# Second product of the experts as seven products of halves in the second and third group, with split weights kept in device memory by the first group

## The chip, the core and the metric

The kernel runs on one core of one Trainium2 chip. The metric is device time in microseconds (us) of one execution. The engines of a core work side by side, each through its own list of instructions in order: TensorE (PE in the profile, with its weight loads shown apart as PEld), VectorE (DVE), ScalarE (ACT), GpSimd (POOL) and SyncE (SP), which here does little more than issue transfers (DMAs). They wait for each other through semaphores.

## The reference, cut to what matters

An attention-like stage without softmax and a three-matrix bilinear stage make `x` (2304 tokens of 512). The last stage, four experts, is what the change is about:

```python
p = domain_probs / (domain_probs.sum(-1, keepdims=True) + 1e-09)
out = np.zeros((N, D), dtype=np.float32)            # N = 2304, D = 512
for e in range(E):                                   # E = 4 experts
    h = np.maximum(x @ w1[e], 0.0)                   # w1[e]: 512 x 1024
    out += p[:, e:e + 1] * (h @ w2[e])               # w2[e]: 1024 x 512
```

All of it is float32. The kernel gets there with three matmuls for each product of two tiles: every operand is split into a high part, rounded to the format that TensorE takes, and a low part, the rest; high x high, high x low and low x high are summed.

## The kernel before

**Tiles.** Everything is cut into tiles of 128 partitions and up to 512 float32 columns (256 KB). 99 such buffers (pool `h`) stay in the core's memory, 5 larger ones (pool `r`, 4 KB a partition) take loads, and 8 banks of 128x512 (pool `b`) take what PE sums.

**The expert stage.** The tokens form three groups `g` = 0, 1, 2 (the first, second and third) of 768 each, as two halves of `W` = 384 tokens or `TILES3` = 3 tiles. For each group, each expert `e` and each `i` = 0..3 there is one step:

- `expert_weights(e, i)` loads 512 KB of each weight matrix (tiles `e1raw`, `e2raw`) and splits them. For `w1` it first makes four sums and differences of quarter blocks (`winograd_weights`, `combined`, line 949; tiles `s12`, `s34`), so that the first product can be done with seven products of halves instead of eight. High parts are casts (line 332, mostly ACT), low parts subtractions (line 337, DVE or POOL).
- `up(g, e, i)` does the first product: seven products of 6 matmuls 128x384, 42 in all. Their results are added up by DVE (tiles `u`, line 1065); `relu` then writes the high part of relu(u) (line 1074) and its low part (line 1086): tiles `ht`.
- `down(g, e, f)` for f = i and f = i + 4 does the second product: for each of 2 x 3 tiles of tokens three matmuls 128x512 (lines 284 to 286), summed over the eight f in six banks. An expert has 8 x 6 x 3 = 144 of these in each group.
- `collect` (line 1145) adds each bank, times the share of the expert, to one of six tiles `acc`; after the last expert `store` writes them out.

All weights are loaded, combined and split anew in each of the three groups.

**The order.** The kernel lists all operations with the engines that could do them and a guessed duration for each. `Plan.order` then walks through a simulated time: each free engine takes, of the operations whose inputs are ready and whose buffers can be had, the one with the lowest stage number, up to `WINDOW` = 14 stages ahead. A stage is one entry of `items`: one `up` or one `down` here, and `mixed(b, f)`, one step of the product ahead of the experts. `down` of a step stands behind `up` of the next. The result fixes the order on each engine; on the chip each engine runs its list in that order.

**Places ahead of the experts.** `mixed` (matmuls `abh,w3oh`) ends in the tiles `xf`; `group_operands(g)` makes from these the 14 split operands `x11`, `x21`, `x22`, `t1` to `t4` of a group (28 tiles).

Of the kernel before, what the change touches and what calls it, by code (L numbers as in the profile page):

```python
# [22 lines left out]
RINGS = {"attention": 9, "decoded": 6}  # L23
WINDOW = 14
WARM = 10
START = 0.7
# [18 lines left out]
class Pair:  # L45
# [7 lines left out]
    def __getitem__(self, at):  # L53
        return self.high[at], self.low[at]


# [164 lines left out]
def attention_moe_kernel(  # L221
# [23 lines left out]


    nc = tc.nc
    B, H, S, D = q.shape
# [51 lines left out]
    def t_pe(n, passes=3):  # L300
        return passes * (0.0137 + n / 2400)

    def load(buf, *parts, key=None, queue="sp", cost=None):
# [11 lines left out]
    def spilled(name, buf):  # L315

        d = Buf("d", name, [P, 512], F32, tag=name)
        add(
            {"sp": 0.73}, lambda _: nc.sync.dma_start(out=d[:, :], in_=buf.tile),
            reads=[buf], writes=[d], latency=2.4,  # L320
        )
        return d

    def whole(t):
        return t

    def split(dst, src, n, to=whole, value=whole, psum=False, key=None):
# [8 lines left out]
        def low(e):  # L336
# [9 lines left out]
            {"dve": t_dve(n)} if psum else {"dve": t_dve(n), "pool": t_pool(n)}, low,  # L346
            reads=[src, (dst.high, key)], writes=[(dst.low, key)], free=psum,
        )

# [640 lines left out]
    def winograd_weights(raw1, full=False):  # L990
# [15 lines left out]
        combined("s4", 256, a12, own(s12, 256), ALU.subtract, [raw1, (s12, 256)], s34, hi)  # L1006
        wa, wb, wc, wd = (Pair("we") for _ in range(4))
        split(wa, raw1, 512, whole, lambda t: t[:, 0])
        if full:
            split(wb, raw1, 512, whole, lambda t: t[:, 1])  # L1010
        else:
            split(wb, raw1, 256, lambda t: t[:, 0:256], lambda t: t[:, 1, 256:512])
        split(wc, s12, 512)
# [5 lines left out]
    def expert_weights(e, i):  # L1019
# [13 lines left out]
        return w, dict(zip(fs, downs))  # L1033

    operands = {}
# [5 lines left out]
    def up(g, e, i):  # L1041
        if g not in operands:
            operands[g] = group_operands(g)
        x = operands[g]
        w, downs = expert_weights(e, i)
        for f, d in downs.items():
            we2[g, e, f] = d

# [19 lines left out]

        def relu(f, part, src):
            s = hts[g, e, f, part] = Pair("ht")  # L1070

# [49 lines left out]
    def down(g, e, f, first, last):  # L1121
# [3 lines left out]
        for i in range(2):  # L1125
            s = hts[g, e, f, i]
            for t in range(TILES3):
# [6 lines left out]
                if last:  # L1134
                    collect(e, *token_tile(g, i, t), ps)

    def collect(e, b, t, ps):
        if e == 0:
# [17 lines left out]
        )  # L1156
        if e < NE - 1:
            return

        def store(_):  # L1160
            if b < B:
# [49 lines left out]
    for b in range(1, NB):  # L1211
        for f in range(KF):
            item(mixed, b, f)
    steps = [(g, e, i) for g in range(len(GROUPS)) for e in range(NE) for i in range(KF // 2)]
    for n, (g, e, i) in enumerate(steps + [(None,) * 3]):
        if g is not None:
            item(up, g, e, i)
        if n:
            g, e, i = steps[n - 1]
            item(down, g, e, i, i == 0, False)  # L1220
            item(down, g, e, i + KF // 2, False, i == KF // 2 - 1)

# [42 lines left out]
```

## Time and profile before

| | |
|---|---|
| time, median of 3 runs | 1158.21 us (1155.22 to 1158.61) |
| the profiled execution: its own time | 1157.3 us |
| its span from the first to the last instruction | 1155.5 us |
| PE busy | 1142.5 us, 99% of the span |
| DVE, ACT, POOL busy | 808.1, 501.8 and 280.7 us |
| moved by DMA | 108.06 MB, mean 94 GB/s |
| PE among the chain of work that ended last | 95% |

The three lines of the second product (284 to 286, 128x512) are the costliest groups on PE. A PE row gives the duration of one matmul from its start to its modelled end; consecutive matmuls overlap, so the pace has to be read from the distance between starts. A row of idle time names what ended it.

### The profile page before, as it was taken

What the parts mean: (1) busy time and instruction counts of PE and PEld (TensorE: products, weight loads), DVE (VectorE), ACT (ScalarE), POOL (GpSimd) and SP (SyncE); (2) the same over time, 40 slices, a digit from 0 to 9 for tenths busy, and PEclk for the clock granted to TensorE, in tenths of its full rate; (3) what the DMA queues carried; (4) which work ended last, traced back from release to release, by engine and by line L of the source; (5) the groups of instructions that cost most, each with busy time, mean ns of one, the idle gap of its engine ahead of it and who ended that gap; (6) DMA issues with size and microseconds to landing.
All of it is one profiled execution on the core that took longest, in us unless ns stands there. A gap on an engine that the chain in (4) does not pass through costs nothing.

```text
span 1155.5 us, 16373 instructions
## 1 busy us (share of the span) xinstructions
PE 1142.5 (99%) x6036; PEld 1011.6 (88%) x6036; DVE 808.1 (70%) x1434; ACT 501.8 (43%) x996; POOL 280.7 (24%) x250
## 2 busy tenths in 40 slices
PE   7999999999999999999999999999999999999998
PEld 6888888888888999989999988999998999998887
DVE  4887787788622676678677886668678987576833
ACT  5776763354434533433335444333333444333210
POOL 3435671033300600001012640001015831010200
PEclk8999999999999999999999999999999999999999
DMA  9996513235200222221121442122120532121001
GB/s 272 330 320 191 172 34 106 75 118 198 85 1 1 82 65 74 73 74 60 55 69 37 128 128 73 41 70 73 55 73 18 166 106 77 55 73 55 1 1 55
DMA packets 108784, 108.06 MB, mean 94 GB/s; under 512 B 13216, under 2 KB 82848, under 8 KB 108704
## 3 DMA queue, kind: packets, MB, share of 16 engines
q1 hardware_dynamic: 107488, 106.75, 29.7%
q8 instruction: 47, 0.77, 0.3%
q10 hardware_dynamic: 1216, 0.26, 0.1%
q14 instruction: 33, 0.27, 0.1%
HBM read 93.88 MB, written 13.11 MB: 93 GB/s over the span
## 4 chain that ended last, share of the span: by engine, by line
PE 95%; DMA 2%; DVE 1%; SPq 0%; ACT 0%; issue 0%; DVEq 0%
PE b L286 31%; PE b L285 30%; PE b L284 30%; PE b L621 2%; PE b L677 1%; PE b L649 1%; DMA kvr<-in_v_dram 1%; DMA kvr<-in_k_dram 1%; DMA w1raw<-in_moe_w_dram 0%; DMA q<-in_q_dram 0%; DVE acc L1145 0%; PE b L714 0%; SPq L306 0%; DVE tl L337 0%; DVE wel L337 0%
## 5 line engine op out<-in xcount | busy, mean ns | idle before, releaser
L1065 DVE TENSOR_TENSOR u<-u,b 128x384 f32<-128x384 f32 x336 | 180.8, 552 | 189.9 <-PE b L286 170.4
L286 PE MATMUL b<-wdh,htl 128*128 128x512 f32 x576 | 225.6, 392 | 0.0
L285 PE MATMUL b<-wdl,hth 128*128 128x512 f32 x576 | 225.4, 391 | 0.0
L284 PE MATMUL b<-wdh,hth 128*128 128x512 f32 x576 | 224.1, 389 | 0.0
L1074 ACT ACTIVATE hth<-u 128x384 fp32r<-128x384 f32 x192 | 100.7, 526 | 221.1 <-DVE u L1065 220.9
L1086 DVE SCALAR_TENSOR_TENSOR htl<-u,hth 128x384 fp32r<-128x384 f32 x192 | 122.2, 640 | 9.9 <-ACT hth L1074 5.0
L609 ACT COPY u<-b 128x384 f32<-128x384 f32 (+1 forms) x76 | 39.6, 521 | 204.1 <-PE b L286 199.5
L286 PEld LDWEIGHTS b<-wdh,htl 128*128 128x128 f32 x576 | 108.0, 188 | 22.7
L285 PEld LDWEIGHTS b<-wdl,hth 128*128 128x128 f32 x576 | 108.1, 188 | 19.1
L284 PEld LDWEIGHTS b<-wdh,hth 128*128 128x128 f32 x576 | 108.2, 188 | 18.9
L332 ACT CAST weh<-s 128x512 fp32r<-128x512 f32 x112 | 68.7, 617 | 43.7 <-DVE s L949 41.1
L337 DVE TENSOR_TENSOR wel<-s,weh 128x512 fp32r<-128x512 f32 x92 | 70.3, 791 | 8.0 <-ACT weh L332 7.0
L337 POOL TENSOR_TENSOR wel<-e1raw,weh 128x256 fp32r<-128x256 f32 (+1 forms) x22 | 37.0, 1681 | 134.8 <-PE b L285 53.5
L337 POOL TENSOR_TENSOR wdl<-e2raw,wdh 128x512 fp32r<-128x512 f32 x17 | 25.3, 1491 | 178.4 <-PE b L286 118.9
L332 ACT CAST wdh<-e2raw 128x512 fp32r<-128x512 f32 x96 | 57.8, 616 | 8.8 <-DMA e2raw<-in_moe_w_dram 6.4
L284 PE MATMUL b<-abh,w3oh 128*128 128x512 f32 (+1 forms) x160 | 59.4, 371 | 0.0
L286 PE MATMUL b<-abh,w3ol 128*128 128x512 f32 (+1 forms) x160 | 58.9, 368 | 0.0
L285 PE MATMUL b<-abl,w3oh 128*128 128x512 f32 (+1 forms) x160 | 58.9, 368 | 0.0
L337 DVE TENSOR_TENSOR wdl<-e2raw,wdh 128x512 fp32r<-128x512 f32 x79 | 55.7, 733 | 0.0
L949 POOL TENSOR_TENSOR s<-e1raw 128x256 f32<-128x256 f32 x29 | 26.0, 906 | 90.6 <-PE b L285 89.2
L337 DVE TENSOR_TENSOR wel<-e1raw,weh 128x256 fp32r<-128x256 f32 (+1 forms) x74 | 47.7, 662 | 0.0
L332 ACT CAST weh<-e1raw 128x512 fp32r<-128x512 f32 x96 | 45.7, 509 | 4.1 <-DMA e1raw<-in_moe_w_dram 2.6
(227 smaller groups left out, 2720.8 us busy)
## 6 DMA issues: line engine op xcount, KB each, us to landing
e1raw<-in_moe_w_dram SPq DMA_DIRECT2D x96, 256.0 KB, 3.2
e2raw<-in_moe_w_dram SPq DMA_DIRECT2D x96, 256.0 KB, 2.9
w3raw<-in_moe_w_dram SPq DMA_DIRECT2D x16, 512.0 KB, 3.8
q<-in_q_dram SPq DMA_DIRECT2D x16, 256.0 KB, 5.8
kv<-in_k_dram SPq DMA_DIRECT2D x16, 256.0 KB, 5.6
kv<-in_v_dram SPq DMA_DIRECT2D x16, 256.0 KB, 5.5
w1raw<-in_moe_w_dram SPq DMA_DIRECT2D x8, 512.0 KB, 6.5
w2raw<-in_moe_w_dram SPq DMA_DIRECT2D x8, 512.0 KB, 6.8
```

What stands on the lines that cost most here:

```text
L284: nc.tensor.matmul(ps, w[0], x[0], start=first, stop=False, skip_group_check=more)
L285: nc.tensor.matmul(ps, w[0], x[1], start=False, stop=False, skip_group_check=more)
L286: nc.tensor.matmul(ps, w[1], x[0], start=False, stop=last, skip_group_check=more)
L332: nc.scalar.copy(to(dst.high.tile), value(src.tile))
L337: (nc.vector if e == "dve" else nc.gpsimd).tensor_tensor(out=to(dst.low.tile), in0=value(src.tile), in1=to(dst.high.tile), op=ALU.subtract)
L609: lambda e: nc.scalar.copy(to(dst.tile), value(src.tile)) if e == "act"
L621: nc.tensor.transpose(ps[:, c], raw[:, c], ident)
L649: nc.tensor.matmul(ps[c, c], a, b_, start=r == 0, stop=r == R)
L949: eng.tensor_tensor(out=t[:, c], in0=x, in1=y, op=op)
L1065: lambda _: nc.vector.tensor_tensor(out=t[:, :W], in0=base[:, :W], in1=ps[:, :W], op=op),
L1074: nc.scalar.activation(out=s.high[:, :W], in_=src[:, :W], func=ACTF.Relu)
L1086: lambda _: nc.vector.scalar_tensor_tensor(out=s.low[:, :W], in0=src[:, :W], scalar=0.0, in1=s.high[:, :W], op0=ALU.max, op1=ALU.subtract,),
```

## The change

In the second and third group (`g` = 1, 2) the second product is done like the first, with seven products of halves instead of eight, and the weights are no longer split there but read back.

- The first group works as before, and also writes its split `w1` tiles to device memory (`spilled`, 7 tiles of 256 KB a step; the two quarter-width parts of one pair now share a tile, `Packed`), and the split parts of `w2` that the seven products need (`keep_w2`, 768 KB a step).
- `w2_sums`, 16 entries set between those of `mixed`, loads `w2` once more, makes its four sums and differences (tiles `t12`, `t34`), splits them and writes them out: 512 KB read and 1 MB written each.
- In the second and third group `kept_weights` reads the 7 tiles `we` of a step back. `relu` works in place on `u` and splits nothing.
- `down_product(g, e, n)`, n = 0..6: reads two buffers `w2` of 512 KB (pool `r`), makes the left operand for the four `i` (`tokens_operand`: up to four sums of `u` tiles a step, and a split of each operand), and runs 3 tiles x 4 i x 3 = 36 matmuls 128x256. Seven of them replace the 144 matmuls 128x512: 252 matmuls of half the width. The four banks stay open over the seven products, and after each product `collect_half` adds three half tiles, 128x256, to `acc`: 21 in place of 6.
- The seven products of an expert are spread over the four `up` steps of the next expert; at the change from the second to the third group three stand ahead of the first `up` (`AHEAD` = 3), and the last seven stand alone at the end.

```diff
+class Packed:
+        self.tile_ = Buf("h", name, [P, 512], F32R)
+    def __getitem__(self, at):
+        _, c = at
+        return self.tile_[:, c], self.tile_[:, c.start + 256:c.stop + 256]
...
@@ def expert_weights(e, i):
         w, _ = winograd_weights(raw1)
+        tiles = [t for pair in dict.fromkeys(pair for pair, _ in w.values()) for t in pair.parts]
+        w1_kept[e, i] = [spilled(f"we{e}_{i}_{n}", t, lambda t: t.bitcast(F32)) for n, t in enumerate(tiles)]
         downs = []
         for n in range(2):
             downs.append(Pair("wd"))
             split(downs[n], raw2, 512, whole, lambda t, n=n: t[:, n])
+            for part, t in enumerate(downs[n].parts):
+                keep_w2(e, i, ((0, 1), (1, 3))[n], part, t)
...
+    W2_OPERANDS = ("b11", "b21", "b22", "t1", "t2", "t3", "-t4")
...
+    def w2_sums(e, i):
+        raw = Buf("r", "e2raw", [P, 2, 512], F32)
+        load(raw, *(
+            (lambda t, n=n: t[:, n], e_w2[e][f * P:(f + 1) * P, :]) for n, f in enumerate((i, i + KF // 2))
+        ))
...
+        combined("t1", 256, part(0, 1), part(0, 0), ALU.subtract, [raw], t12, lo)
+        combined("t2", 256, part(1, 1), own(t12, 0), ALU.subtract, [raw, (t12, 0)], t12, hi)
+        combined("t3", 256, part(1, 1), part(0, 1), ALU.subtract, [raw], t34, lo)
+        combined("-t4", 256, part(1, 0), own(t12, 1), ALU.subtract, [raw, (t12, 256)], t34, hi)
+        for t, which in ((t12, (3, 5)), (t34, (5, 7))):
+            s = Pair("wt")
+            split(s, t, 512)
+            for n, p in enumerate(s.parts):
+                keep_w2(e, i, which, n, p)
+    def kept_weights(e, i):
+        for d in w1_kept[e, i]:
+            t = Buf("h", "we", [P, 512], F32R)
+            load(t, (lambda t: t.bitcast(F32), d))
...
@@ def up(g, e, i):
-        w, downs = expert_weights(e, i)
+        if g:
+            w = kept_weights(e, i)
+        else:
+            w, downs = expert_weights(e, i)
...
         def relu(f, part, src):
+            if g:
+                h32[g, e, f, part] = src
+                add(
+                    {"act": t_act(W), "dve": t_fast(W)},
+                    lambda eng: nc.scalar.activation(out=src[:, :W], in_=src[:, :W], func=ACTF.Relu)
...
+                return
...
+    PRODUCTS = [
+        ("a11", "b11", 0, True, [(0, 0)]),
+        ("a12", "b21", 1, True, [(0, 0)]),
+        ("s2", "t2", 0, False, [(0, 1)]),
+        ("s1", "t1", 1, True, [(1, 1)]),
+        ("s3", "t3", 0, False, [(1, 1)]),
+        ("s4", "b22", 1, False, [(0, 1)]),
+        ("a22", "-t4", 0, False, [(1, 0)]),
+    ]
...
+    def down_product(g, e, n):
+        left, right, at, start, targets = PRODUCTS[n]
+        if n == 0:
+            yacc[g, e] = [[bank(), bank()] for _ in range(2)]
+        banks = yacc[g, e][at]
...
+        for i0 in range(0, KF // 2, 2):
+            raw = Buf("r", "w2", [P, 2, 2, 256], F32R)
+            add(
+                {"sp": 1.46},
+                lambda _, raw=raw, i0=i0: nc.sync.dma_start(out=raw.tile.bitcast(F32), in_=kept.tile[:, k, i0:i0 + 2]),
+                reads=[kept], writes=[raw], latency=2.4,
+            )
...
+            def mms(_, t=t, ps=ps, c=c):
+                for i, (h, (raw, r)) in enumerate(zip(lefts, rights)):
+                    mm3(
+                        ps[:, c], h[:, t * P:(t + 1) * P], (raw[:, r, 0], raw[:, r, 1]),
+                        start and i == 0 and t % 2 == 0, i == KF // 2 - 1, True,
+                    )
...
+    for g in range(1, len(GROUPS)):
+        for e in range(NE):
+            if e == 0 and g > 1:
+                for late in waiting[:AHEAD]:
+                    item(*late)
+                waiting = waiting[AHEAD:]
+            for i in range(KF // 2):
+                item(up, g, e, i)
+                n = -(-len(waiting) // (KF // 2 - i))
+                for late in waiting[:n]:
+                    item(*late)
+                waiting = waiting[n:]
+            waiting = [(down_product, g, e, n) for n in range(len(PRODUCTS))]
+    for late in waiting:
+        item(*late)
```

**On PE, second group, behind an `up` step** (names: `x22`, an operand of the group; `wd`, split `w2`; `ht`, split tokens; `b`, a bank). Before:

```order
L286 MATMUL b_8835<-x22h_6511,wel_8577 128x384
L284 MATMUL b_8847<-wdh_8122,hth_8656 128x512
L285 MATMUL b_8847<-wdl_8425,hth_8656 128x512
L286 MATMUL b_8847<-wdh_8122,htl_8667 128x512
L284 MATMUL b_8854<-wdh_8122,hth_8656 128x512
```

After:

```order
L300 MATMUL b_9317<-x22h_7141,we_9119 128x384
L298 MATMUL b_9328<-w2_9123,hth_8883 128x256
L299 MATMUL b_9328<-w2_9123,hth_8883 128x256
L300 MATMUL b_9328<-w2_9123,htl_9063 128x256
L298 MATMUL b_9328<-w2_9123,hth_8890 128x256
L299 MATMUL b_9328<-w2_9123,hth_8890 128x256
L300 MATMUL b_9328<-w2_9123,htl_9067 128x256
L298 MATMUL b_9328<-w2_9145,hth_8997 128x256
```

The matmuls are half as wide, and a bank's tile is now finished over the four `i` at once before the next tile begins.

**On SP, where the third group begins** (`we`, a kept `w1` tile read back; `w2`, a kept operand of `w2`; the waits are named: PE for a buffer that PE still reads, DMAHW for the transfer eight places ahead, DVE and Pool for buffers that these read). Before:

```order
L306 DMA e2raw_8721<-in_moe2_w2_dram 128x512 [waits DMAHW6_49,DVE_49,Pool_49]
L306 DMA e2raw_8721<-in_moe2_w2_dram 128x512 [waits DMAHW7_49]
L306 DMA e1raw_8778<-in_moe2_w1_dram 128x4x128 [waits DMAHW0_49,Activation_49,Pool_49]
L306 DMA e1raw_8778<-in_moe2_w1_dram 128x4x128 [waits DMAHW1_49]
L306 DMA e2raw_8897<-in_moe2_w2_dram 128x512 [waits DVE_49,DMAHW2_49,Activation_49,Pool_49]
```

After:

```order
L323 DMA we_10043<-we0_1_2_4650 128x512 [waits DMAHW2_49,PE_49]
L1309 DMA w2_10083<-w2kept3_4065 128x1024 [waits DMAHW3_49,PE_49]
L1309 DMA w2_10102<-w2kept3_4065 128x1024 [waits DMAHW4_49,PE_49]
L1309 DMA w2_10145<-w2kept3_4065 128x1024 [waits DMAHW5_49,PE_49]
L1309 DMA w2_10168<-w2kept3_4065 128x1024 [waits DMAHW6_49,PE_49]
L323 DMA we_10188<-we0_1_3_4619 128x512 [waits DMAHW7_49,Pool_49]
L323 DMA we_10193<-we0_1_4_4663 128x512 [waits DMAHW0_49,DVE_49]
```

Loads of raw weights, which waited for the engines that split them, are replaced by loads of finished operands, and most of these wait for PE.

**On DVE, where the operands of the third group are finished** (`x..l`, `t.l`, low parts of the operands; `u` takes the sums of the up product). Before, ahead of the last `up` step of the second group:

```order
L337 TENSOR_TENSOR t3l_9075<-t3_8935,t3h_9023 128x384
L337 TENSOR_TENSOR t4l_9086<-t4_9040,t4h_9050 128x384
L949 TENSOR_TENSOR t1_9097<-xf_4106 128x256
L949 TENSOR_TENSOR t1_9097<-xf_4287 128x128
L337 TENSOR_TENSOR x11l_9105<-xf_4106,x11h_8734 128x256
L1065 TENSOR_TENSOR u_9126<-u_9103,b_9090 128x384
```

After, directly ahead of the first `up` step of the third group:

```order
L1350 SCALAR_TENSOR_TENSOR acc_7874<-b_10110,pn_74,acc_7874 128x256
L351 TENSOR_TENSOR x11l_10262<-xf_4601,x11h_9854 128x128
L351 TENSOR_TENSOR x21l_10270<-xf_4436,x21h_9883 128x256
L351 TENSOR_TENSOR x21l_10270<-xf_4617,x21h_9883 128x128
L351 TENSOR_TENSOR x22l_10282<-xf_4436,x22h_9891 128x256
L351 TENSOR_TENSOR x22l_10282<-xf_4617,x22h_9891 128x128
L351 TENSOR_TENSOR t1l_10294<-t1_10212,t1h_10230 128x384
L351 TENSOR_TENSOR t2l_10300<-t2_10234,t2h_10252 128x384
L351 TENSOR_TENSOR t3l_10311<-t3_10254,t3h_10260 128x384
L351 TENSOR_TENSOR t4l_10313<-t4_10257,t4h_10267 128x384
L1166 TENSOR_TENSOR u_10341<-u_10296,b_10317 128x384
```

The operands were finished within the last step of the second group; now the second half of them stands behind that group's products, next to the matmuls that read them.

## Rows read from the trace of the kernel before

**Rows 1.** The page, part 1: busy us (share of the span), instructions.
```profile
PE 1142.5 (99%) x6036; PEld 1011.6 (88%) x6036; DVE 808.1 (70%) x1434; ACT 501.8 (43%) x996; POOL 280.7 (24%) x250
```

**Rows 2.** The page, part 4: the chain that ended last, by engine.
```profile
PE 95%; DMA 2%; DVE 1%; SPq 0%; ACT 0%; issue 0%; DVEq 0%
```

**Rows 3.** Waits of PE, longest in total first: us, times, longest.
```profile
PE b L649 <- DMA kv<-in_v_dram: 2.6, 2, 2.0
```

**Rows 4.** PE in time, last downs: first and last of 57 matmuls 128x512.
```profile
1137.09 0.39 PE L284 MATMUL b<-wdh,hth 128*128 128x512 f32 x1
...
1149.78 0.39 PE L286 MATMUL b<-wdh,htl 128*128 128x512 f32 x1
```

**Rows 5.** PE in time, end of `mixed`: first and last of 96 matmuls 128x256.
```profile
391.45 0.28 PE L284 MATMUL b<-abh,w3oh 128*128 128x256 f32 x1
...
402.84 0.28 PE L286 MATMUL b<-abh,w3ol 128*128 128x256 f32 x1
```

**Rows 6.** PE in time, first `up`: first and last of 42 matmuls 128x384.
```profile
402.96 0.34 PE L284 MATMUL b<-x11h,weh 128*128 128x384 f32 x1
...
410.07 0.33 PE L286 MATMUL b<-x22h,wel 128*128 128x384 f32 x1
```

**Rows 7.** DVE groups by line and shape: count, busy us, mean ns, idle before.
```profile
L1086 DVE SCALAR_TENSOR_TENSOR htl<-u,hth 128x384 fp32r<-128x384 f32 x192 | 122.2, 640 | 9.9 <-ACT hth L1074 5.0
L337 DVE TENSOR_TENSOR wel<-s,weh 128x512 fp32r<-128x512 f32 x92 | 70.3, 791 | 8.0 <-ACT weh L332 7.0 <-PE b L285 0.8
L337 DVE TENSOR_TENSOR wdl<-e2raw,wdh 128x512 fp32r<-128x512 f32 x79 | 55.7, 733 | 0.0
L1145 DVE SCALAR_TENSOR_TENSOR acc<-b,pn,acc 128x512 f32<-128x512 f32 x54 | 36.7, 740 | 13.2 <-PE b L286 13.2
L949 DVE TENSOR_TENSOR s<-e1raw 128x256 f32<-128x256 f32 x67 | 28.4, 441 | 0.0
...
L337 DVE TENSOR_TENSOR t1l<-t,t1h 128x384 fp32r<-128x384 f32 x4 | 2.2, 552 | 0.0
...
L584 DVE SCALAR_TENSOR_TENSOR xrl<-b,g,xrh 128x256 fp32r<-128x256 f32 x4 | 1.7, 478 | 1.0 <-ACT xrh L577 1.0
```

**Rows 8.** ACT groups by line and shape.
```profile
L1074 ACT ACTIVATE hth<-u 128x384 fp32r<-128x384 f32 x192 | 100.7, 526 | 221.1 <-DVE u L1065 220.9
...
L332 ACT CAST wdh<-e2raw 128x512 fp32r<-128x512 f32 x96 | 57.8, 616 | 8.8 <-DMA e2raw<-in_moe_w_dram 6.4 <-issue 2.1 <-PE b L285 0.2
...
L332 ACT CAST t2h<-t 128x384 fp32r<-128x384 f32 x6 | 3.1, 512 | 0.1
```

**Rows 9.** POOL group of the same shape.
```profile
L337 POOL TENSOR_TENSOR t1l<-t,t1h 128x384 fp32r<-128x384 f32 x2 | 2.2, 1110 | 0.0
```

**Rows 10.** Stretches: us, busy PE, PEld, DVE, ACT, POOL; clock, DMA share, GB/s.
```profile
300.00:350.00 50.00, 50.00 (x231) 41.57 (x230) 15.52 (x24) 17.41 (x34) 5.08 (x5) 1.00 0.04 11
350.00:400.00 50.00, 50.00 (x256) 42.87 (x255) 24.12 (x65) 22.44 (x55) 12.93 (x3) 1.00 0.11 33
900.00:950.00 50.00, 50.00 (x253) 45.35 (x252) 44.45 (x65) 24.06 (x49) 32.90 (x30) 1.00 0.43 137
```

**Rows 11.** The page, parts 2 and 3: DMA rate in 40 slices; the main queue.
```profile
DMA  9996513235200222221121442122120532121001
GB/s 272 330 320 191 172 34 106 75 118 198 85 1 1 82 65 74 73 74 60 55 69 37 128 128 73 41 70 73 55 73 18 166 106 77 55 73 55 1 1 55
...
q1 hardware_dynamic: 107488, 106.75, 29.7%
```

**Rows 12.** The page, part 6: DMA issues, KB each, us to landing.
```profile
e1raw<-in_moe_w_dram SPq DMA_DIRECT2D x96, 256.0 KB, 3.2
...
w3raw<-in_moe_w_dram SPq DMA_DIRECT2D x16, 512.0 KB, 3.8
...
w2raw<-in_moe_w_dram SPq DMA_DIRECT2D x8, 512.0 KB, 6.8
```

**Rows 13.** SP in time: the issue of two transfers.
```profile
402.33 0.82 SPq L306 DMA_DIRECT2D e2raw<-in_moe_w_dram  x2
```

**Rows 14.** All engines in time: the last collects, the last stores.
```profile
1146.81 4.15 DVE L1145 SCALAR_TENSOR_TENSOR acc<-b,pn,acc 128x512 f32<-128x512 f32 x6 [10.58 <-PE b L286]
...
1151.32 1.12 SPq L1167 DMA_DIRECT2D out_dram<-acc  x2
```

More of the change, by code (lines that the diff above doesn't have):

```diff
@@ L1006, in winograd_weights @@
         combined("s4", 256, a12, own(s12, 256), ALU.subtract, [raw1, (s12, 256)], s34, hi)
-        wa, wb, wc, wd = (Pair("we") for _ in range(4))
+        wa, wc, wd = (Pair("we") for _ in range(3))
+        wb = Pair("we") if full else Packed("we")
         split(wa, raw1, 512, whole, lambda t: t[:, 0])
@@ L1011, in winograd_weights @@
         else:
-            split(wb, raw1, 256, lambda t: t[:, 0:256], lambda t: t[:, 1, 256:512])
+            split_packed(wb, raw1, lambda t: t[:, 1, 256:512])
         split(wc, s12, 512)
@@ L1044, in up @@
         x = operands[g]
[L1045 to L1047 removed]
+        if g:
+            w = kept_weights(e, i)
+        else:
+            w, downs = expert_weights(e, i)
+            for f, d in downs.items():
+                we2[g, e, f] = d
         def times(ps, a, b):
@@ L1135, in down, with tokens_operand, sum_of, get @@
                     collect(e, *token_tile(g, i, t), ps)
+    h32 = {}
+    sums = {}
+    PRODUCTS = [
[7 more added lines that the diff above has]
+    ]
+    def tokens_operand(g, e, name, i):
+        a = {
+            f"a{part + 1}{k + 1}": h32[g, e, i + k * KF // 2, part] for part in range(2) for k in range(2)
+        }
+        def sum_of(name, x, y, op):
+            t = sums[g, e, name, i] = half(name)
+            add(
+                {"dve": t_dve(W), "pool": t_pool(W)},
+                lambda eng: (nc.vector if eng == "dve" else nc.gpsimd).tensor_tensor(
+                    out=t[:, :W], in0=x[:, :W], in1=y[:, :W], op=op
+                ),
+                reads=[x, y], writes=[t],
+            )
+            return t
+        def get(name):
+            if name in a:
+                return a[name]
+            if (g, e, name, i) in sums:
+                return sums[g, e, name, i]
+            x, y, op = {
+                "s1": ("a21", "a22", ALU.add), "s2": ("s1", "a11", ALU.subtract),
+                "s3": ("a11", "a21", ALU.subtract), "s4": ("a12", "s2", ALU.subtract),
+            }[name]
+            return sum_of(name, get(x), get(y), op)
+        s = Pair("ht")
+        split(s, get(name), W, lambda t: t[:, :W], lambda t: t[:, :W])
+        return s
@@ new lines, in collect_half, with emit @@
+    def collect_half(g, e, part, t, column, ps, c, n):
+        b, tile_at = token_tile(g, part, t)
+        new = e == 0 and (b, tile_at, column) not in begun
+        if (b, tile_at) not in accs:
+            accs[b, tile_at] = half("acc")
+        begun.add((b, tile_at, column))
+        a = accs[b, tile_at]
+        to = slice(column * 256, column * 256 + 256)
+        def emit(eng):
+            sc = pn[:, b * R + tile_at, e:e + 1]
+            if not new:
+                nc.vector.scalar_tensor_tensor(
+                    out=a[:, to], in0=ps[:, c], scalar=sc, in1=a[:, to], op0=ALU.mult, op1=ALU.add
+                )
+            elif eng == "act":
+                nc.scalar.activation(out=a[:, to], in_=ps[:, c], func=ACTF.Copy, scale=sc)
+            else:
+                nc.vector.tensor_scalar(out=a[:, to], in0=ps[:, c], scalar1=sc, scalar2=None, op0=ALU.mult)
+        add(
+            {"act": t_act(256, True) + 0.1, "dve": t_dve(256)} if new else {"dve": t_dve(256) + 0.06}, emit,
+            reads=[(ps, t), share], writes=[(a, column)], free=True,
+        )
+        if e == NE - 1 and (part, column, n) in ((0, 1, 5), (1, 0, 6)):
+            store_tile(b, tile_at, a)
@@ L1213, in attention_moe_kernel @@
             item(mixed, b, f)
[L1214 to L1221, printed above, removed]
+            n = (b - 1) * KF + f
+            if n % 3 < 2 and n // 3 * 2 + n % 3 < 16:
+                n = n // 3 * 2 + n % 3
+                item(w2_sums, n // 4, n % 4)
+    waiting = []
+    for e in range(NE):
+        for i in range(KF // 2):
+            item(up, 0, e, i)
+            for late in waiting:
+                item(*late)
+            waiting = [
+                (down, 0, e, i, i == 0, False), (down, 0, e, i + KF // 2, False, i == KF // 2 - 1),
+            ]
+    for g in range(1, len(GROUPS)):
+        for e in range(NE):
+            if e == 0 and g > 1:
+                for late in waiting[:AHEAD]:
+                    item(*late)
+                waiting = waiting[AHEAD:]
+            for i in range(KF // 2):
+                item(up, g, e, i)
[4 more added lines that the diff above has]
+            waiting = [(down_product, g, e, n) for n in range(len(PRODUCTS))]
+    for late in waiting:
+        item(*late)
     for stage, (fn, args) in enumerate(items):
```

86 lines of the change are left out of this document (80 added, 6 removed).

## Prediction

> **What bounds the kernel now.** The first view is the share of each engine on the page [rows 1]: PE is busy 1142.5 of 1155.5 us, with DVE next at 808.1. The second is the chain of work that ended last: 95% of it is PE [rows 2]. The third is the list of PE's waits: the longest in total is 2.6 us, for a load of the attention stage, not one of the experts [rows 3]. So PE sets the time, and in the expert stage it does nothing but matmuls. The question is what these cost, read as distances between starts, and not as the 0.39 or 0.28 us that a row gives to one, since consecutive ones overlap.
>
> - 128x512: 56 distances from 1137.09 to 1149.78 make 0.2266 us each [rows 4].
> - 128x256: 95 distances from 391.45 to 402.84 make 0.1199 us each [rows 5].
> - 128x384: 41 distances from 402.96 to 410.07 make 0.1734 us each [rows 6].
>
> The difference between the first two, 0.1067 us for 256 columns, is a column at 2.4 GHz, and the granted clock is 1.00 in all windows read [rows 10]. What is left, 0.1199 - 0.1067 = 0.0132 us, is a fixed part of each matmul. By these paces an `up` takes 42 x 0.1734 = 7.28 us, a `down` step (36 matmuls 128x512) 8.16 us and one of the new products (36 matmuls 128x256) 4.32 us. The 48 steps of before come to 48 x 15.44 = 741.1 us; the stage lasted from 402.96 [rows 6] to 1149.78 + 0.23 [rows 4], that is 747.0 us. Only 5.9 us, 0.12 a step, are lost to waiting.
>
> **The change part by part.**
>
> *PE's work.* For each expert in the second and third group 144 x 0.2266 = 32.63 us go and 252 x 0.1199 = 30.21 us come: -2.42 us, eight times: **-19.3 us**. Both paces hold one weight load for every matmul (as many PEld as PE instructions [rows 1]), which the new products need too. The gain is thin: with 12.5% fewer columns but 75% more matmuls, the fixed part eats 108 x 0.0132 = 1.4 of 3.8 us. It would be gone at a pace of 32.63/252 = 0.1295 us.
>
> *Work of the other engines in these two groups.* DVE loses 128 lows of `relu` at 640 ns (81.9 us), 36 collects at 740 (26.6), 53 lows `wdl` at 733 (38.8), 82 wide lows `wel` at 791 (64.9), and about 22 narrow lows and 90 sums of `w1` at 441 (49.4): 262 us. It gains 144 half collects (taken as 478 ns, the nearest row that reads a bank at this width: 68.8), 71 sums of `u` and 114 lows of operands at 552 (102.1): 171 us. So DVE is relieved by 91 us [rows 7]. ACT exchanges 128 casts of `relu` at 526, 64 casts `wdh` at 616 and the casts of `w1` for 128 relus and 224 operand casts at 512 (114.7 us): about even [rows 8]. POOL takes 57 sums and 110 lows, each 1.11 us [rows 9], 185 us, and loses some 80 operations; its share goes from 24% to about 35%. No engine comes near PE. This costs nothing while work is ahead of need; lateness is priced below.
>
> *Loads.* In these groups the step loads 7 x 256 KB of `we`, and each product 2 x 512 KB: 58.7 + 58.7 = 117.4 MB, where before raw weights made 33.6 MB. By the paces the two groups last 32 x 15.44 = 494 us now and 475 after, so the demand is 247 GB/s. Queue q1 moved 106.75 MB in 29.7% of 1155.5 us: 311 GB/s while busy; the busiest slices show 320 and 330 [rows 11]. So it fits at 79% of that, if transfers can be in flight most of the time. SP's issue, 0.41 us each [rows 13], makes 42 x 0.41 = 17 us for an expert of some 59 us: no bound. A `we` tile has its buffer two thirds of a step or more ahead of use; 256 KB land in about 3.2 us [rows 12]. The `w2` buffers are fewer: five, shared, so the second half of a product's operands is asked for when the product two places ahead ends. Where an `up` lies between, that leaves 12 us. Where products stand back to back (the change to the third group, the end) it leaves 4.32 + 0.72 = 5.0 us. Against that, 512 KB landed in 3.8 us, or in 6.8 among all the loads of the start [rows 12]; with the issue, 4.2 or 7.2. At the end nothing else is loaded, so 3.8 is the nearer row and the cost is 0; at the change of groups `we` loads run too, and three products could each lose 2.2 us: 0 to 7.
>
> *Operands of a product.* Each product waits for four sums, four casts and four lows. The last sums follow the expert's last `up`, but the products are spread over the next expert's steps and the first two need no sum, so time is there. I price lateness of operands and loads together at **+1 us**: bounds -4 (most of the 5.9 us of small waits disappear with the split of weights) and +8 (the loads above, and a little for operands).
>
> *Start of the third group.* Before, its operands were finished within the last step of the second group. After, their lows, about eight instructions of 0.4 to 0.55 us [rows 7], some 4 us, stand on DVE behind the last collect ahead of the first `up`; with sums and lows queued ahead of them it is up to 9 us. PE has one product of 4.32 us as cover. Stall 0 to 6 us, taken as **+3**. The second group's start is unchanged.
>
> *First group and `mixed`.* A step of the first group writes 2.6 MB and loads 1.05 MB in 15.44 us, 238 GB/s, again below 311. The writes wait for the splits, and the buffers for the writes. `w2_sums` adds DVE 51 x 0.441 + 27 x 0.733 = 42 us, ACT 32 x 0.616 = 20 us and some 19 us of POOL. In the last 100 us of `mixed` DVE is busy 39.6 us, ACT 39.9, POOL 18.0 [rows 7, 8, 10]; with it 82, 60 and 37. It fits, but DVE may be late now and then: 0 to +6, taken as **+1**.
>
> *Tail.* The last collects go at 4.15 / 6 = 0.69 us each, with the last store behind them [rows 14]; the last one is now of half width: **-0.3** (-0.5 to 0).
>
> Sum: -19.3 + 1 + 3 + 1 - 0.3 = **-14.6 us**, against the profiled execution 1157.3 - 14.6 = 1142.7. The median of the runs, 1158.2, lies 0.9 us above that execution; predicted median **1143.6 us**. All low ends together give -23.8 and 1134.4; all high ends +0.7 and 1158.9.
>
> **Rivals.**
>
> *Nothing is late (full saving).* The start of the third group is covered and the small waits shrink: -19 to -24 us, 1134 to 1139. For it: DVE is relieved by 91 us. Against: the lows of the third group stand visibly close to the matmuls that read them.
>
> *Operands lag (no change).* Each product needs more steps in a row (sum, cast, low), and half of the lows are on POOL at 1.11 us where DVE takes 0.55 [rows 7, 9]. If half of that difference, 0.28 us, is waited for at each of 56 products, 15.7 us go, and -15.6 from the other terms becomes 0: 1158.3. From 0.22 us a product the gain falls below 0.3%, which is about what a measurement can tell from no change. Against: before, the same kind of chain behind `relu` costs 0.12 us a step or less.
>
> *The loads become the bound (slower).* Place: the second and third group. Before, the queue there moves 40 to 170 GB/s [rows 11], so a sustained 247 is not shown in this stage. Transfers wait for buffers that PE frees, and eight at most are outstanding. The other terms give 1141.7 with these groups at 475 us; slower by 0.3% needs 494 us, which 117.4 MB take at 238 GB/s, that is 76% of 311. It decides from there. The first six slices of the page, in which loads are also held up by buffers, average 220 GB/s; at that rate the groups take 534 us, 1141.7 + 59 + 0.9 = 1201. Against: 320 and 330 in two of these slices, and leads of 10 us and more.
>
> *Narrow matmuls run slower here (slower).* If the fixed part doubled, for operands that change with every matmul, the pace would be 0.1331 us: 2016 x 0.1331 = 268.3 against 1152 x 0.2266 = 261.0, +7.3 in place of -19.3, and 1170. Against: the row of `mixed` has the same form, three matmuls of changing high and low parts, over 95 of them [rows 5].
>
> The Trainium skill (TensorE: Matmul & The Clock Gate, Back-to-back issue gap) gives the sustained spacing of pairs of weight load and matmul as 81 ns at N=128 and 131 ns at N=512; about 98 ns at 256 would be an estimate from that page. By that, an expert would go from 144 x 131 = 18.9 to 252 x 98 = 24.7 us, and the change would lose some 47 us. This trace disagrees with the page at both widths, 0.2266 at 512 and 0.1199 at 256 [rows 4, 5], and the measurement decides.
>
> That the change does not do what it says is excluded by the built program, which has 2016 matmuls 128x256 in these groups.
>
> **How the numbers follow.** Forecast, 1139.5 to 1151: 0.66. Full saving: 0.14. Operands lag, 1151 to 1162, half of it within 0.3%: 0.09. Loads bound: 0.08. Narrow pace: 0.03. Faster by over 0.3% (below 1154.7): 0.66 + 0.14 + 0.045 = 0.85. Slower (above 1161.7): 0.11. Within: 0.04. The range from 1136 to 1156 holds the forecast, most of the full saving and about half of the lag: 0.66 + 0.10 + 0.05 = 0.81.
>
> **What would show it.** The pace of 128x256 in the products, from starts: 0.120, with 4.3 us for 36; 0.13 or more would refute the main term. Steps of the second group: 7.3 + 8.2 x 0.93 = 14.8 us on average. PE's waits before the first `up` of the third group: some 3 us, ended by DVE. Waits of PE ended by DMA `w2` or `we`: a few us in all; if they come to 20 us, with DMA busy above 8 tenths throughout, the loads bound and the prediction is wrong. Waits ended by POOL lows of `htl`: below 0.2 us a product. The stage `mixed` should end within 2 us of its present 403.

## Result and the profile after

| | before | changed |
|---|---|---|
| time, median | 1158.41 us (1155.22 to 1159.59) | 1138.91 us (1138.42 to 1139.94) |
| ratio | | 0.9837, 95% interval 0.9816 to 0.9858 |
| the profiled execution, its span | 1157.3, 1155.5 us | 1139.9, 1137.8 us |
| PE busy, matmuls | 1142.5 us, 6036 | 1119.7 us, 6900 |
| DVE, ACT, POOL busy | 808, 502, 281 us | 795, 523, 386 us |
| moved by DMA | 108 MB | 259 MB |

19.5 us less, where 14.6 were forecast: inside the range, 4.7 us below the predicted time, and in the interval that the text gave to the rival of the full saving. It did not get there in that rival's way, as the account below shows.

The page of the changed kernel, parts 1 to 3, answers to [rows 1] and [rows 11]:

```profile
PE 1119.7 (98%) x6900; PEld 1035.1 (91%) x6900; DVE 795.3 (70%) x1435; ACT 522.5 (46%) x1071; POOL 385.9 (34%) x358
...
DMA  9996512334689899676767823867678768586746
GB/s 268 306 340 195 187 39 93 93 102 142 201 272 354 270 343 349 230 240 221 239 208 236 322 95 131 287 229 278 211 240 313 250 199 298 207 275 243 242 164 207
...
q1 hardware_dynamic: 164320, 257.78, 68.0%
```

From the 26th slice on, the loads of the second and third group keep DMA at 4 to 8 tenths and some 240 GB/s on average. PE does not wait for them: this is its list of waits (line, what it waited for: us in total, times, longest), as in [rows 3]:

```profile
PE b L679 <- DMA kv<-in_v_dram: 5.8, 3, 3.7
PE b L679 <- DMA kvr<-in_v_dram: 2.5, 2, 1.4
PE b L299 <- DVE x11l L351: 1.9, 1, 1.9
...
PE b L298 <- DVE u L1166: 0.5, 1, 0.5
```

No `w2`, no `we` and no `htl` stands in it. The only wait in the expert stage of more than 0.5 us is for `x11l`, a low part of the third group's operands. PE in time (start us, duration) shows the paces. First an expert of the second group, from the first `up` of one to that of the next; then the first and the last matmul of the eight products at the end, 288 in all:

```profile
743.19 0.34 PE L298 MATMUL b<-x11h,we 128*128 128x384 f32 x1
...
802.52 0.34 PE L298 MATMUL b<-x11h,we 128*128 128x384 f32 x1
...
1098.64 0.28 PE L298 MATMUL b<-w,hth 128*128 128x256 f32 x1
...
1133.07 0.28 PE L300 MATMUL b<-w,htl 128*128 128x256 f32 x1
```

287 distances from 1098.64 to 1133.07 make 0.1200 us, as read from `mixed` [rows 5]. A step takes (802.52 - 743.19) / 4 = 14.83 us; forecast were 14.8.

**Where the 17.7 us between the two spans lie.** The expert stage begins, in its first `up`, at 402.96 us before and here:

```profile
404.75 0.34 PE L298 MATMUL b<-x11h,weh 128*128 128x384 f32 x1
```

- Ahead of it: +1.8 us, all of it ahead of `mixed`, which lasts 136.7 us in both. Most of it stands in one wait for attention loads (`kv`), in a part that both programs share. The other profiles here begin the stage anywhere from 402.3 to 404.9 us, the changed kernel's second one at 402.3, so this is no cost of the change.
- From the first `up` to the last matmul: 746.8 us before, 728.3 after, -18.5.
- Behind the last matmul: 5.7 us before, 4.7 after, -1.0.

The -18.5 are -19.3 by the paces, +3.7 at the third group's start (below), +0.7 at one wait for `u` in the first group, and -3.6 that the forecast did not have.

**The third group's start.** PE there, in time (the bracket is idle time and what ended it):

```profile
875.34 0.34 PE L298 MATMUL b<-x11h,we 128*128 128x384 f32 x1
877.61 0.41 PE L299 MATMUL b<-x11l,we 128*128 128x384 f32 x1 [1.93 <-DVE x11l L351]
...
878.72 0.53 PE L298 MATMUL b<-x21h,we 128*128 128x384 f32 x1
879.04 0.53 PE L299 MATMUL b<-x21l,we 128*128 128x384 f32 x1
...
881.28 0.53 PE L300 MATMUL b<-t1h,we 128*128 128x384 f32 x1
881.60 0.41 PE L298 MATMUL b<-t2h,we 128*128 128x384 f32 x1
```

One distance is 2.27 instead of 0.17 us. Then some ten are 0.32 us, which is 384 columns at 1.2 GHz, the lower level of the clock: another 1.6 us. The stretch of these, as in [rows 10], has a granted clock of 0.50:

```profile
878.40:881.60 3.20, 3.20 (x11) 3.20 (x11) 2.95 (x7) 0.36 (x1) 1.95 (x1) 0.50 0.98 355
```

On DVE at the same time:

```profile
874.90 1.43 DVE L979 TENSOR_TENSOR t<-xf 128x256 f32<-128x256 f32 x2
876.25 0.61 DVE L979 TENSOR_TENSOR t<-t,xf 128x256 f32<-128x256 f32 x2
876.79 0.47 DVE L1350 SCALAR_TENSOR_TENSOR acc<-b,pn,acc 128x256 f32<-128x256 f32 x1
877.18 0.28 DVE L351 TENSOR_TENSOR x11l<-xf,x11h 128x128 fp32r<-128x128 f32 x1
```

`x11l` ends at 877.46 and the matmul starts 0.15 us later: combinations and a collect stand ahead of it on DVE, as the order of the change showed.

### The profile page after: what moved, and what is told of

It is laid out like the page before. It is cut to its first block, busy times and chain, and to the rows that moved or that the text cites. A ratio compares the mean times of both kernels' runs of the same rounds, so it can differ in the third digit from the quotient of the medians.

```text
span 1137.8 us, 19512 instructions
## 1 busy us (share of the span) xinstructions
PE 1119.7 (98%) x6900; PEld 1035.1 (91%) x6900; DVE 795.3 (70%) x1435; ACT 522.5 (46%) x1071; POOL 385.9 (34%) x358
## 4 chain that ended last, share of the span: by engine, by line
PE 93%; DMA 3%; DVE 2%; SPq 1%; issue 1%; ACT 0%; POOL 0%; ACTq 0%; DVEq 0%
PE b L298 30%; PE b L299 30%; PE b L300 30%; PE b L651 2%; DMA kvr<-in_v_dram 2%; PE b L707 1%; SPq L323 1%; PE b L679 1%; DMA e2raw<-in_moe_w_dram 0%; DMA w<-w2kept 0%; PE b L744 0%; SPq L336 0%; DVE t L979 0%; DMA w2kept<-wdh 0%; DVE tl L351 0%
## 5 line engine op out<-in xcount | busy, mean ns | idle before, releaser
L300 PE MATMUL b<-w,htl 128*128 128x256 f32 x672 | 190.1, 283 | 0.0
L299 PE MATMUL b<-w,hth 128*128 128x256 f32 x672 | 190.0, 283 | 0.0
L298 PE MATMUL b<-w,hth 128*128 128x256 f32 x672 | 189.9, 283 | 0.0
L1350 DVE SCALAR_TENSOR_TENSOR acc<-b,pn,acc 128x256 f32<-128x256 f32 x144 | 66.9, 480 | 96.9 <-PE b L300 96.4
L300 PEld LDWEIGHTS b<-w,htl 128*128 128x128 f32 x672 | 128.8, 192 | 0.0
L299 PEld LDWEIGHTS b<-w,hth 128*128 128x128 f32 x672 | 128.7, 192 | 0.0
L298 PEld LDWEIGHTS b<-w,hth 128*128 128x128 f32 x672 | 128.7, 191 | 0.0
L1175 ACT ACTIVATE u<-u 128x384 f32<-128x384 f32 x128 | 67.3, 526 | 116.9 <-DVE u L1166 116.3
L351 POOL TENSOR_TENSOR htl<-s,hth 128x384 fp32r<-128x384 f32 x60 | 64.3, 1080 | 123.7 <-ACT hth L346 86.3
L300 PE MATMUL b<-wdh,htl 128*128 128x512 f32 x192 | 75.3, 392 | 0.0
L299 PE MATMUL b<-wdl,hth 128*128 128x512 f32 x192 | 75.2, 392 | 0.0
L298 PE MATMUL b<-wdh,hth 128*128 128x512 f32 x192 | 74.7, 389 | 0.0
L1186 ACT ACTIVATE hth<-u 128x384 fp32r<-128x384 f32 x64 | 33.6, 525 | 74.2 <-DVE u L1166 74.2
```

What stands on the lines that cost most here:

```text
L298: nc.tensor.matmul(ps, w[0], x[0], start=first, stop=False, skip_group_check=more)
L299: nc.tensor.matmul(ps, w[0], x[1], start=False, stop=False, skip_group_check=more)
L300: nc.tensor.matmul(ps, w[1], x[0], start=False, stop=last, skip_group_check=more)
L351: (nc.vector if e == "dve" else nc.gpsimd).tensor_tensor(out=to(dst.low.tile), in0=value(src.tile), in1=to(dst.high.tile), op=ALU.subtract)
L1175: lambda eng: nc.scalar.activation(out=src[:, :W], in_=src[:, :W], func=ACTF.Relu)
L1186: nc.scalar.activation(out=s.high[:, :W], in_=src[:, :W], func=ACTF.Relu)
```

## Experiments

The kernel before and those compared with it ran on the same chip each time; 1158.0, 1158.3, 1158.1 and 1157.8 us are its medians in the four sets.

**Weights kept, product as before (e1_kept_only).** `w2_sums` and the products are gone; the split `w2` tiles are kept and read back too:

```diff
             w = kept_weights(e, i)
+            for f in (i, i + KF // 2):
+                we2[g, e, f] = kept_down(e, f)
...
-                item(w2_sums, n // 4, n % 4)
```

> The weights are kept in device memory by the first group and read back in the second and third, but the second product stays as before, 144 matmuls 128x512 for each expert and group; the sums of w2 and the seven products are not there. Theory A (the gain of the change is PE's arithmetic, and keeping the weights alone gives none): PE's work is that of before, so 1154 to 1160 us. Rival B (the gain comes from the splits that no longer load DVE, ACT and POOL in these groups): 1139 to 1148 us. The run also tells what made the wide matmuls of before take 0.2285 us on average in the expert stage and only 0.2266 in the last 57: if it is the splitting beside them, their pace in the second and third group falls to 0.2266 and the time to about 1154; if not, it stays at 0.2285 and the time at 1157 to 1160.

Measured: 1157.56 us, ratio 0.9995 (0.9986 to 1.0005). Theory A holds. DVE falls from 808.1 to 670.7 us and this buys nothing:

```profile
PE 1139.9 (99%) x6036; PEld 1009.0 (87%) x6036; DVE 670.7 (58%) x1205; ACT 405.7 (35%) x804; POOL 176.6 (15%) x159
```

Its wide matmuls take 0.2283 us on average over the 1727 distances of the stage, against 0.2285 before; in the two groups that no longer split they take 0.2282, against 0.2285 there before. So the splits beside them make at most a fifth of what keeps these above the 0.2266 of the last 57 [rows 4].

**The halving without the saved product (e5_halves).** On top of e1, each matmul 128x512 of these groups becomes two:

```diff
-                    mm3(ps.tile, s[:, t * P:(t + 1) * P], w[:, :], first, last)
...
+                    for n, c in enumerate((slice(0, 256), slice(256, 512))):
+                        mm3(ps[:, c], s[:, t * P:(t + 1) * P], w[:, c], first and n == 0, last, True)
```

> As e1_kept_only (weights kept, all eight products), but in the second and third group each matmul 128x512 of the second product is made as two of 128x256: the halving without the saved product. Theory A (fixed cost of each matmul, from the paces 0.2285 and 0.1199): 8 x (288 x 0.1199 - 144 x 0.2285) = 8 x (34.53 - 32.90) = +13 us, at most 1.7 us less if the up steps beside narrow matmuls keep their faster pace, so 1168 to 1171 us. Rival (narrow matmuls cost nothing extra in a stream, so the whole saving of the seven products is columns, and the pace of 0.1199 in the products is made by something else): 1158 us.

Measured: 1169.27 us, ratio 1.0095 (1.008 to 1.011). The halving alone costs 11.7 us over e1: theory A, at the end where the `up` steps beside narrow matmuls run faster. The stage in its first and last matmul:

```profile
403.12 0.34 PE L298 MATMUL b<-x11h,weh 128*128 128x384 f32 x1
...
1161.26 0.28 PE L300 MATMUL b<-wdh,htl 128*128 128x256 f32 x1
```

These are 758.1 us for 2016 x 0.1734 + 576 x 0.2266 + 2304 x 0.1199 = 756.3, or 1.8 us over the paces of [rows 4 to 6]; before, the stage was 5.7 us over them. So most of that excess goes when the wide matmuls go. From e5 to the changed kernel PE loses the eighth product: 8 x 36 x 0.1199 = 34.5 us, less the 3.7 at the third group's start, 30.8; measured 1169.27 - 1138.91 = 30.4. The other engines' work and the order of the matmuls differ between the two as well, but PE waits for them nowhere else than listed above.

**`w1` split anew in every group (e2_w1_split_again).** The first group no longer writes `w1` out either:

```diff
...
-            w = kept_weights(e, i)
+            w = split_weights(e, i)
```

> As the changed kernel, but w1 is loaded raw, combined and split in every group as before, and not kept; w2 is kept and the seven products stay. Moved by DMA: about 259 - 29 - 59 + 17 = 188 MB, DVE about 100 us more. Theory A (PE sets the time; keeping w1 is not what gives the gain): the time of the changed kernel, 1137 to 1142 us. Rival (the operands of the products need the time on DVE and POOL that keeping w1 frees): 1146 us or more, with waits of PE for u, htl or we.

Measured: 1147.54 us, ratio 0.9915 (0.9900 to 0.9930). The rival's number, but its mechanism at one place only: inside the groups PE waits for next to nothing (0.5 us for `htl` in all), although DVE is busy 43 of 50 us. Stretches of 50 us (busy PE, PEld, DVE, ACT, POOL; granted clock, DMA share, GB/s), one within the second group and the one with the change of groups:

```profile
750.00:800.00 50.00, 50.00 (x363) 50.00 (x362) 43.27 (x77) 26.56 (x57) 28.21 (x27) 1.00 0.53 169
850.00:900.00 50.00, 40.09 (x275) 39.77 (x274) 42.30 (x94) 20.45 (x43) 31.74 (x22) 0.90 0.45 143
```

Nearly all is lost at the third group's start, in one wait and the slow matmuls behind it:

```profile
PE b L300 <- DVE wel L351: 9.9, 1, 9.9
```

With these, 12.3 us go there, against 3.7 in the changed kernel: the 8.6 us between the two times. Keeping `w1` is worth that much in this order of the work, at one place.

**The operands of the third group earlier (e3_early3, e9_early3, e9_early2, e10_half_early).**

```diff
...
+                if (g, e, i) == (1, NE - 1, 3):
+                    item(early_operands, 2)
                 item(up, g, e, i)
```

> As the changed kernel, but the operands of the third group are listed ahead of the last up step of the second group, so that DVE finishes them before that step's sums. Theory (PE's wait of about 2 us for x11l and the some 10 matmuls at half the clock behind it, 1.6 us, both come from the late operands): both go, 1135 us, granted clock 1.00 in the stretch 850 to 900 us. Rival (the 4 us of work on DVE only move the lateness to the second group's last products): 1138 to 1141 us, with a wait of PE elsewhere.

Measured: 1136.14 us, ratio 0.9816 (0.9801 to 0.9831). Most of the theory: no wait for `x11l` and no half clock, but part of the lateness moved, as the rival had it:

```profile
PE b L298 <- DVE u L1169: 1.6, 2, 1.1
```

The same beside the changed kernel on one chip:

> The changed kernel itself once more, as the mark for the two kernels with earlier operands on the same chip: 1138 to 1140 us, with 2 us of wait and 1.6 us of half clock at the third group's start.

> e3_early3 once more beside the changed kernel. Theory (the third group's start costs 3.8 us in the changed kernel, and 1.6 us of wait for u are what comes in its place): 2.2 us below the changed kernel, 1136 to 1137 us. Rival (the difference of e3_early3 was that of two chips or days): equal within 0.5 us.

Measured: 1137.31 (0.9822, 0.9807 to 0.9837) and 1136.13 us (0.9810, 0.9796 to 0.9825). The gain is 1.2 us here, between the theory's 2.2 and the rival's 0.5, and 2.4 by the ratios of the two earlier sets; the profiles, free of what lies ahead of the experts, have 727.5 and 726.2 us for the stage. It has the lowest time of the versions run, but its interval overlaps that of the changed kernel: that it is faster is likely, not shown.

> As e3_early3, but the operands of the third group are listed one up step earlier, ahead of the last but one of the second group. Theory (the 1.6 us left in e3_early3 are waits for sums of u behind the operands on DVE, and an earlier place only moves them): 1136 to 1138 us, with a wait of some 1 to 2 us one step earlier. Rival (spread over two steps, the operands fit in between): no wait, 3.8 us below the changed kernel, 1134.5 to 1135.5 us.

Measured: 1143.76 us, ratio 0.9877 (0.9860 to 0.9893), 6.5 us above the changed kernel. Neither number: the wait is one step earlier, as the theory said, but 3.8 us long, with half clock behind it, and waits for `htl` (1.2 us) and for a load of `we` (0.8 us) follow:

```profile
842.05 0.67 PE L298 MATMUL b<-t1h,we 128*128 128x384 f32 x1 [3.79 <-DVE u L1169]
842.52 0.52 PE L299 MATMUL b<-t1l,we 128*128 128x384 f32 x1
842.84 0.52 PE L300 MATMUL b<-t1h,we 128*128 128x384 f32 x1
```

The last of these lists only half of the operands early (`kk` = 0):

> As the changed kernel, but the half of the third group's operands that belongs to the first two of the four blocks of 128 rows of w1 (DVE finishes it at 872 us in the changed kernel) is listed ahead of the last up step of the second group, the other half stays at the group's start. Theory (the operands' work on DVE is too much for one place, as the changed kernel shows at 875 us with 1.9 us and e9_early3 at 856 us with 1.0 us of wait, and fits in two): no wait of PE at either place and no stretch at half clock, 3.6 us below the changed kernel, 1133.5 to 1135 us. Rival (each half still delays sums of u or of the products): waits of 1 to 2 us stay, 1136 to 1138 us.

Measured: 1136.74 us, ratio 0.9829 (0.9814 to 0.9843). The rival: the half clock is gone, waits of 0.8 us (`htl`) and 0.7 (`u`) stay, at two places. None of the three other places tried is free of waits; two of them have shorter ones than the changed kernel.

**The same move with `w1` split anew (e7_split_early3).** The edit of e3_early3 on e2.

> e2_w1_split_again with the operands of the third group listed ahead of the last up step of the second group. Theory A (keeping w1 is worth only what the third group's start costs without it, a wait of 10 us and 2.2 us of half clock): the wait at about 874 us goes or shrinks to 2 us, 1136 to 1140 us. Rival (at the change of groups DVE has too much to do in any order, sums of u, operands and w1 lows together): the wait moves but stays, 1145 to 1149 us.

Measured: 1150.12 us, ratio 0.9935 (0.9914 to 0.9956). Theory A falls and the rival holds, 1 us above its range: the wait moved from 874 to 849 us, into the last `up` of the second group, and is still 9.4 us. DVE there:

```profile
851.39 1.15 DVE L979 TENSOR_TENSOR t<-xf 128x256 f32<-128x256 f32 x4
...
856.56 0.54 DVE L351 TENSOR_TENSOR t4l<-t,t4h 128x384 fp32r<-128x384 f32 x1
857.02 0.74 DVE L979 TENSOR_TENSOR s<-e1raw 128x256 f32<-128x256 f32 x2
857.70 0.41 DVE L979 TENSOR_TENSOR s<-s,e1raw 128x256 f32<-128x256 f32 x1
858.03 0.67 DVE L351 TENSOR_TENSOR wel<-e1raw,weh 128x512 fp32r<-128x512 f32 x1
```

The lows of `w1` for the next `up`, on which PE waits, now stand behind all operands of the third group. Whether another place would do was not tried.

**Reserve behind PE (e4_two, e4_one).** One or two of the three matmuls of each pair are left out, and nothing else.

> As the changed kernel, but the seven products of the second and third group leave out the matmul of high tokens with low weights, 672 of the 2016 matmuls 128x256; all loads, sums and splits stay. A look at the reserve behind PE. Theory A (loads and other engines have reserve for it): 672 x 0.1199 = 80.6 us less, 1058 us; the loads then run at 117.4 MB in about 394 us = 298 GB/s. Rival (the loads end at some 240 to 260 GB/s, close to where they are now): the second and third group stay above 450 us, 1115 us or more.

Measured: 1064.68 us, ratio 0.9193 (0.9175 to 0.9212), 74.2 us below the changed kernel of the 80.6 expected. The rival falls. Of the 6.4 us missing, 4.5 lie at the third group's start, where the same wait is 5.7 us; loads cost 0.3. The second fence has 100 us of the second group, with 298 GB/s and PE busy throughout (over the two groups, 645 to 1058 us, the mean is 271 GB/s):

```profile
PE b L299 <- DVE x11l L351: 5.7, 1, 5.7
...
PE b L1322 <- DMA w<-w2kept: 0.3, 1, 0.3
```

```profile
700.00:800.00 100.00, 100.00 (x682) 99.89 (x680) 75.52 (x139) 48.29 (x106) 41.31 (x37) 1.00 0.85 298
```

> As the changed kernel, but the seven products keep only the matmul of high tokens with high weights, 672 of 2016; all loads, sums and splits stay. If PE still set the time: 161 us less, 978 us, with loads at 117.4 MB in 314 us = 374 GB/s, above the 340 to 354 of any slice so far. Expected is another bound: loads at 311 to 340 GB/s give 345 to 378 us for the two groups, 1010 to 1042 us in all; if DVE, with its 300 us of work in these groups and the port it shares, comes first, a like time with DVE at 9 tenths and DMA below 8.

Measured: 1015.40 us, ratio 0.8768 (0.8750 to 0.8785), inside the interval expected. Two of its stretches of 25 us:

```profile
750.00:775.00 25.00, 24.70 (x160) 24.18 (x159) 22.98 (x43) 13.51 (x31) 14.69 (x14) 1.00 0.98 356
800.00:825.00 25.00, 13.70 (x74) 12.45 (x75) 25.00 (x53) 12.08 (x27) 17.53 (x19) 0.80 1.03 391
```

DVE and the DMA engines are both full or nearly so there, so no single next bound can be named. PE's longest waits are for `acc` (7.3 us), `u` (6.3), `x11l` (6.2) and the loads `w` (5.2). The loads deliver 356 and 391 GB/s in these two stretches, and 306 on average over the two groups.

**Products in the first group too (e6_all_products).** All of `w2` is made into operands by 16 steps, `w1` is split in every group, operands stand early:

```diff
-    for g in range(1, len(GROUPS)):
+    for g in range(len(GROUPS)):
...
+                if g == 0 and e < 2:
+                    item(w2_sums, e + 2, i)
```

> Seven products in the first group too: all operands of w2 are made and kept by the 16 steps on w2 (8 of them in the mixed stage, 8 in the first group), w1 is split anew in each group, and the operands of the next group are listed ahead of the last up step of a group. Theory A (PE sets the time in every group): 576 x 0.2285 = 131.6 us become 1008 x 0.1199 = 120.9, some 1.5 us of slower steps go and the 3.8 us at the third group's start, so 1120 to 1126 us. Rival (the first group, which splits w1 and w2 and writes w2 while it makes operands for products, becomes bound by DVE, POOL or the loads): 1132 us or more, with waits of PE between 400 and 640 us.

Measured: 1173.12 us, ratio 1.0139 (1.0117 to 1.0161), slower than before. PE's work is 712 us by the paces, as theory A reckoned, but the stage lasts 760.9:

```profile
PE b L300 <- DVE wel L351: 23.0, 5, 10.7
PE b L298 <- ACT hth L346: 5.2, 6, 2.3
PE b L300 <- DVE htl L351: 4.6, 8, 2.3
```

Two of the waits for `wel`, 10.7 and 9.4 us, are in the last `up` step ahead of the two changes of groups, the pattern of e7, each with matmuls at the lower clock behind it; some 16 us are lost from 426 to 506 us, in the first group, where `w1` and `w2` are split. PE waits there for `wel` (2.6 us) and, once the products have begun, for their operands (`htl` 3.6, `hth` 2.4); much of the rest are matmuls at the lower clock behind these waits. This run changes several things at once; it shows where they break, and not which one is to blame for each wait.

## Why the prediction came out right

- **PE's work, -19.3 us.** The mechanism is shown, in both parts: halving costs 11.7 us, the eighth product gives 30.4. The pace of narrow matmuls is 0.1200 as read, and the rival of a narrow pace falls with it. The size was off by 3.6: the wide pace of 0.2266 came from the last 57 matmuls, while over the whole stage it is 0.2285, and `up` beside them takes 0.1747 instead of 0.1734 per matmul. 1152 x 0.0019 + 1344 x 0.0013 = 3.9 us more to save. The loss of some 47 us, an estimate from the Trainium skill's figures (TensorE: Matmul & The Clock Gate, Back-to-back issue gap), did not come: this trace, with 0.1200 us at 128x256, does not agree with it.
- **"5.9 us lost to waiting."** This is the step that failed. PE's list of waits had nothing of this in the expert stage; the 5.9 us were the difference between a pace read at one place and the mean of the stage: 1727 x 0.0019 + 2016 x 0.0013 = 5.9. e1 shows that they are for the most part not the splits', e5 that most of them go with the wide matmuls. Why wide matmuls between `up` steps take 1% longer stays open. The forecast had them as a bound of -4 under lateness, and took +1.
- **Lateness of operands and loads, +1.** 0 in the groups: not one wait for `htl`, `w` or `we`. The rival of lagging operands falls, and e2 shows with how much reserve: DVE at 43 of 50 us, and still one wait of 0.5 us within a group. The relief of DVE was half of what the text said, 47 us and not 91: in the second and third group (before, then after, as in [rows 10]) DVE is busy 357 and 310 us. The text took off 82 wide lows `wel` where the trace has 72, and priced at 552 ns 114 lows of operands that took 706 to 728 ns. It cost nothing, since DVE was not the bound.

```profile
645.00:1150.00 505.00, 505.00 (x2526) 456.37 (x2524) 356.97 (x635) 188.41 (x372) 109.77 (x100) 1.00 0.22 69
646.00:1133.00 487.00, 485.07 (x3398) 483.13 (x3397) 309.75 (x585) 197.32 (x428) 188.31 (x176) 1.00 0.67 231
```

- **Loads as the bound.** The demand came out at some 240 GB/s, as forecast (247), and is met. e4 shows the supply: 298 GB/s over 100 us in which PE never waits, 391 at most over 25 us. The 311 GB/s that the text took as the limit, from the busy share of the whole run, was too low.
- **Third group's start, +3 (0 to 6).** 3.7 us, by the engine and the instruction named. But 1.6 of it are the lower clock behind the wait, which was in no step of the working; the wait itself is 2.1. So the 3.7 comes near the 3 in part by luck. The wait is also why the full saving's own reason, that the start is covered, does not hold.
- **First group and `mixed`, +1.** `mixed` lasts as long as before to 0.1 us, the first group loses 0.7. In `mixed` some 26 MB more went through (260 GB/s on average where 67 stood), and DVE was busy 107 us where it had been 71, in a stretch that had room.
- **Tail, -0.3.** -1.0. The last collect is half as wide, 0.48 us where one took 0.69; what the rest of the 1.0 is was not taken apart.

With the terms as measured: -19.3 - 3.6 + 3.7 + 0.7 - 1.0 = -19.5, the difference of the medians. The -3.6 is what the other terms leave of the stage's difference in one pair of profiles, and the +1.8 ahead of the stage is left out as scatter, so that this sum meets the medians to 0.1 is partly chance.

## What to carry to other kernels

Where one engine is busy all the time, price a change by distances between starts of its own instructions, and read these in the stage and the neighbourhood that the change removes, not at a quiet end: that difference, 1% of a pace, was a fifth of this gain. Seven products for eight pay only if the narrower tiles do not eat it: here 34.5 us saved against 11.7 paid. Look for the cost of such a change at the seams, where one group ends and the next begins: in every variant here that makes the seven products, long waits stood at or just ahead of a seam, where work of two groups meets on DVE. Moving this work ahead gave back a third of the 3.7 us by the medians on one chip, or cost 6.5 us.

## What the runs showed of the hardware

- A wait of PE can cost nearly twice its length. Behind 1.9 us of waiting for `x11l`, ten matmuls 128x384 took 0.32 us each (granted clock 0.50, 1.2 GHz) before 0.17 came back; behind 3.8 us in e9_early2 and 9.9 us in e2 the same. Behind the wait of some 1 us in e3_early3 the next distances were 0.28 and then 0.17. Short waits can do it too where several stand close together: in e6 PE waited six times for 0.2 to 0.7 us between 463 and 468 us, and the granted clock from 467 to 471 us was 0.57.
- One core's loads ran at 356 and 391 GB/s over the two stretches of 25 us of e4_one; no slice of the kernel before shows more than 330.
- DVE's lows of 128x384 took 728 ns on average here, against 545 for the same shape among the operands `t1l`:

```profile
L351 DVE TENSOR_TENSOR htl<-s,hth 128x384 fp32r<-128x384 f32 x68 | 49.0, 728 | 5.2 <-ACT hth L346 4.4 <-PE b L299 0.5
...
L351 DVE TENSOR_TENSOR t1l<-t,t1h 128x384 fp32r<-128x384 f32 x5 | 2.7, 545 | 0.0
```

POOL does the other half of these lows, at 1080 ns. In the trace, the 31 of the 68 that ran while POOL was idle took 552 ns on average and none over 559; the 37 beside which POOL was busy took 875, up to 1414, but ten of these no more than 560. So the slow ones all stand beside work of POOL, though not all work of POOL slows them; no run without that work was made.
